# Attention with head mixing and two dense layers: transfer queues of the start, product with v and first dense products moved

## The chip, the cores and the metric

The kernel runs on one core of one Trainium2 chip. The metric is the device time of one execution in microseconds (us); lower is better. TensorE (PE in the profile) has two clock levels, 1.2 and 2.4 GHz; the profile gives the granted clock of a stretch as a share of the higher one.

## The reference

Attention over 2 batches, 12 heads, 448 positions and 64 values per head, with the scores mixed across heads before the softmax and the weights mixed across heads after it; then two dense layers on 896 tokens of 768 values.

```python
scores = scale * np.matmul(q, k.transpose(0, 1, 3, 2))
scores = np.einsum('bhij,hg->bgij', scores, w_pre)
scores = scores - np.max(scores, axis=-1, keepdims=True)
attn = np.exp(scores)
attn = attn / (np.sum(attn, axis=-1, keepdims=True) + 1e-09)
attn = np.einsum('bhij,hg->bgij', attn, w_post)
return np.matmul(attn, v)
...
a = x @ w_a
b = x @ w_b
x = a * b @ w_out
h = x @ w_in
r = np.maximum(h, 0.0)
return (r * r) @ w_out
```

## The kernel before, in words

**Tiles and slots.** A batch is cut into four query tiles of 120, 120, 120 and 88 rows. The scores of a tile are computed per pair of heads (`qk`, line 172) into PSUM, copied to SBUF by ScalarE for even heads and VectorE for odd heads (`qk_copy`, lines 182 and 184), and then moved by transfers from SBUF to SBUF into the buffer `G[t % 2]` (`spread`, lines 192 and 195), where one partition holds one head of one of ten query rows. The attention proper runs in slots of two such groups of rows: six slots for a tile of 120 rows, five for one of 88, 46 slots in all. A slot mixes the heads (`premix`, line 215, out of G), takes the row minimum on VectorE (`smin`, 223) and the exponential on ScalarE (`sexp`, 231), scales the second mixing matrix (`weights2`, 242 to 244), multiplies with it (`post`, 263), and copies the result from PSUM into the tile's buffer A (`evac`, 286 on ScalarE and 284 on VectorE). The product with v (`av`, 298) reads the whole A of a tile, twelve heads in six steps of 16 matmuls; `av_out` (308) copies it to SBUF.

**Order.** The order of every queue is the order of the program text (a manual schedule). In turn n of the slot loop come premix of slot n+1, post of slot n, softmax of slot n+1, evac of slot n, weights2 of slot n+1, then the lists `dve_l` (pieces of the splitting of dense weights) and `mid` (score products of the next tile, splitting of q, k and x, loads, and `av`). The six steps of `av` of a tile lie in the slots of the next tile: two in its second slot, then one a slot. `load_v` of batch 1 stands behind the last `av` of batch 0, and v has one buffer.

**Start.** Tiles 0 and 1 of batch 0 have their scores computed ahead of the loop. Tile 0's scores go to G[0] in three portions, limits GS = (0, 2, 6, 12) groups of rows: transfers of 35, 70 and 105 KB per head. The first two portions are issued by ScalarE's queue (even heads) and SyncE's (odd heads), the third by GpSimd's and SyncE's. Tile 1's scores are staged in `a0`, a tile of the pool "a" (two buffers), and go to G[1] in one transfer of 210 KB per head; each `A[b, t]` is the next tile of the same pool and tag. G[1] is cleared by GpSimd in one memset (322).

**End of attention.** Six steps of the first dense block (each three matmuls, lines 519 to 521) run behind the slot loop, then `attention_tail`: `av` of the last tile, with one PSUM bank "av", and the splitting of batch 1's x (465, 466). The dense part follows.

Of the kernel before, what the change touches and what calls it, by code (L numbers as in the profile page):

```python
# [7 lines left out]
F32 = mybir.dt.float32  # L8
# [7 lines left out]
B, H, S, D = 2, 12, 448, 64  # L16
DM = H * D
# [4 lines left out]
ROW = 2 * KG  # L22
TILE = 120
ROWS = (120, 120, 120, 88)
OFFS = (0, 120, 240, 360)
NTL = 4
PK = 13
GP = 128
JP = 112
NJ = S // JP  # L30
NC = DM // 128
NF1 = DFF1 // 128
NF2 = DFF2 // 128
# [26 lines left out]
def attention_moe_kernel(  # L60
# [18 lines left out]
    def ps(tag):  # L79
        return psum.tile([128, 512], F32, tag=tag, name=tag, bufs=PB[tag])  # L80
# [21 lines left out]
    sb = att.enter_context(tc.tile_pool(name="att", bufs=1))  # L102
    s_p = att.enter_context(tc.tile_pool(name="s", bufs=4))
    e_p = att.enter_context(tc.tile_pool(name="e", bufs=2))
    a_p = att.enter_context(tc.tile_pool(name="a", bufs=2))

    G = [sb.tile([128, H, S], F32, name=f"G{i}") for i in range(2)]
    A = {}
# [43 lines left out]
        qp[b, t] = (hi, lo)  # L152

    def load_v(b, eng=nc.sync):
        x = sb.tile([JP, NJ, DM], F32, tag="v", name="v")
        eng.dma_start(out=x, in_=v[b])
        vv[b] = x

# [28 lines left out]
    def spread(t, h, s, r0, r1, eng=nc.sync):  # L187
        g = G[t % 2]
        n = r1 - r0
        o = r0 * ROW  # L190
        last = ROW - 1 if h == H - 1 else ROW
        eng.dma_start(out=g[h:PK * (last - 1) + h + 1:PK, r0:r1, :], in_=s[o:o + last * n])
        if last < ROW:
            a = place(last, h)
            eng.dma_start(out=g[a:a + 1, r0:r1, :], in_=s[o + last * n:o + ROW * n])
# [15 lines left out]
    def premix(b, m):  # L211
        t, r, n = PAIRS[m]
        for i in range(n):
            p = ps("T")
            nc.tensor.matmul(  # L215
                p[0:GP, 0:S], wpre_sb[0:GP, 0:GP], G[t % 2][0:GP, r + i, :], start=True, stop=True
            )
            Tps[b, m, i] = p

    def smin(b, m, i):  # L220
        if i == 0:
            NB[b, m] = e_p.tile([128, 2], F32, tag="nb", name="nb")
        nc.vector.tensor_reduce(  # L223
            out=NB[b, m][0:GP, i:i + 1], in_=Tps[b, m, i][0:GP, 0:S], op=ALU.min, axis=AX.X
        )

    def sexp(b, m, i):
        if i == 0:
            Z[b, m] = e_p.tile([128, 2], F32, tag="z", name="z")
        e = e_p.tile([128, S], F32, tag=f"e{i}", name="e")  # L230
        nc.scalar.activation(  # L231
            out=e[0:GP], in_=Tps.pop((b, m, i))[0:GP, 0:S], func=ACTF.Exp, bias=NB[b, m][0:GP, i:i + 1], scale=-1.0,
            accum_out=Z[b, m][0:GP, i:i + 1],
        )
        E[b, m, i] = e

    def weights2(b, m):
        n = PAIRS[m][2]
        z = Z.pop((b, m))[0:GP, 0:n]
        NB.pop((b, m))  # L240
        w2 = e_p.tile([128, 2, H * KG], F32, tag="w2", name="w2")
        nc.vector.tensor_scalar(z, z, 1e-9, None, ALU.add)
        nc.vector.reciprocal(out=z, in_=z)
        nc.vector.tensor_tensor(  # L244
            out=w2[0:GP, 0:n, :],
            in0=wp[0:GP].rearrange("p (o g) k -> p o (g k)", o=1).to_broadcast([GP, n, H * KG]),
            in1=z.rearrange("p (n o) -> p n o", o=1).to_broadcast([GP, n, H * KG]), op=ALU.mult,
        )
        W2[b, m] = w2
# [39 lines left out]
    def av(b, t, c):  # L289
        n = ROWS[t]  # L290
        if c % 2 == 0:
            AVp[b, t] = ps("av")
        p = AVp[b, t]
        o = (c % 2) * TILE
        for j in range(NJ):
            for e in range(2):
                g = 2 * c + e
                nc.tensor.matmul(  # L298
                    p[64 * e:64 * e + 64, o:o + n], vv[b][:, j, g * D:(g + 1) * D], A[b, t][:, j * H + g, 0:n],
                    start=(j == 0), stop=(j == NJ - 1), skip_group_check=True,  # L300
                )
# [17 lines left out]
    nc.vector.memset(G[0][:, GS[1]:GS[2], :], 0.0)  # L319
    nc.gpsimd.dma_start(out=wp, in_=wpost)  # L320
    nc.gpsimd.memset(G[0][:, GS[2]:GS[3], :], 0.0)
    nc.gpsimd.memset(G[1], 0.0)
    nc.vector.tensor_scalar(wpre_sb, wpre_sb, -0.125, None, ALU.mult)


# [8 lines left out]
    a0 = a_p.tile([128, NJ * H, TILE], F32, tag="a", name="a0").rearrange("p g i -> p (g i)")  # L334
    stage1 = [a0[0:TILE, h * S:(h + 1) * S] for h in range(H)]
    tags0 = (("qk", "qk"), ("T", "T"), ("post", "post"))
    hw = (nc.scalar, nc.sync)
    for c in range(NC):
        qk(0, 0, c, tags0[c % 3])
        while Sps:  # L340
            _, t, h, p = Sps.pop(0)
            qk_copy(t, h, p, stage0[h])
            spread(0, h, stage0[h], GS[0], GS[1], hw[h % 2])
    for h in range(H):
        spread(0, h, stage0[h], GS[1], GS[2], hw[h % 2])
    load_q(0, 2)
    for h in range(H):
        spread(0, h, stage0[h], GS[2], GS[3], (nc.gpsimd, nc.sync)[h % 2])
    for c in range(NC):
        qk(0, 1, c, tags0[c % 3])  # L350
        while Sps:
            _, t, h, p = Sps.pop(0)
            qk_copy(t, h, p, stage1[h])
    for h in range(H):
        spread(1, h, stage1[h], 0, ROWS[1] // ROW, (nc.gpsimd, nc.sync)[h % 2])
    load_v(0)
    busy(4)

# [3 lines left out]
    span = [sum(1 for x in PAIRS if x[0] == t) for _, t in tiles]  # L362
    base = [sum(span[:i]) for i in range(len(tiles))]
    NS = len(plist)
    act_l, dve_l, mid = {}, {}, {}

    def at(d, slot, *f):
        d.setdefault(max(slot, 0), []).append(f)
# [3 lines left out]
    for ti, (b, t) in enumerate(tiles):  # L372
        s0, sp = base[ti], span[ti]
        if ti + 1 < len(tiles):
            nxt = tiles[ti + 1]
            for c in range(NC if ti else 0):
                at(mid, s0 - 3 + c, qk, *nxt, c)
            if ti + 2 < len(tiles):
                if ti:
                    at(mid, s0 - 2, load_q, *tiles[ti + 2])  # L380
                at(mid, s0 + 1, split_q, *tiles[ti + 2])
            if nxt[1] == NTL - 1 and nxt[0] + 1 < B:
                for i in range(2):
                    at(mid, s0 - 4, load_k, nxt[0] + 1, i)
                for c in range(NC):
                    at(mid, s0 - 2 + c, split_k, nxt[0] + 1, c)
        if ti > 0:
            pb, pt = tiles[ti - 1]
            for c in range(NC):
                s = s0 + 1 + (c * (sp - 1)) // NC  # L390
                at(mid, s, av, pb, pt, c)
                if c % 2:
                    at(mid, s, av_out, pb, pt, c // 2)
            if pt == NTL - 1 and pb + 1 < B:
                at(mid, s0 + sp, load_v, pb + 1)


    NU = w.shape[0]
# [54 lines left out]
    def split_w(u):  # L453
        if u < NU:
            todo.extend(split_steps(u))
# [19 lines left out]

    s0 = base[-1]
    s1 = base[-2]
    at(mid, s1 - 1, load_w, 0)
    at(mid, s1 - 1, load_w, 1)
    at(mid, s1 + 1, split_w, 0)  # L480
    at(mid, s1 + 1, split_w, 1)
    for i in range(12):
        at(dve_l, s1 + 1 + (2 * i) // 3, steps, 1)
    for i in range(NC):
        at(mid, s0 - 1 + (2 * i) // 3, split_x0, i)

    def run(d, n):
        for f in d.get(n, []):
            f[0](*f[1:])

    def softmax(n):
        b, m = plist[n]
        for i in range(PAIRS[m][2]):
            smin(b, m, i)
            sexp(b, m, i)

    premix(*plist[0])
    softmax(0)
    weights2(*plist[0])
    for n in range(NS):  # L500
        if n + 1 < NS:
            premix(*plist[n + 1])
        qk_out()
        post(*plist[n])
        if n + 1 < NS:
            softmax(n + 1)
        run(act_l, n)
        evac(*plist[n], 0)
        evac(*plist[n], 1)
        if n + 1 < NS:  # L510
            weights2(*plist[n + 1])
        run(dve_l, n)
        run(mid, n)
    run(mid, NS)

    def mm(p, u, s, x, first, last):
        hi, lo = whl[u]
# [2 lines left out]
        nc.tensor.matmul(p[:, 0:S], hi[:, sl], x[1], start=False, stop=False)  # L520
        nc.tensor.matmul(p[:, 0:S], lo[:, sl], x[0], start=False, stop=last)  # L521

    tags = ["qk", "T", "post", "av", "qk", "T", "post", "T"]
    tcnt = [0]

    def nps():
# [1 line left out]
        return ps(tags[(tcnt[0] - 1) % 8])  # L528

    soon = []  # L530

    def hook():
        if soon:
            soon.pop(0)()
        else:
            steps(1)


    def stage(u0, order, K, src, consume, first=None):
        acc = {}  # L540
        left = {}
        for u, _ in order:
            left[u] = left.get(u, 0) + 1
        for n, (u, b) in enumerate(order):
            for s in range(US):
                m, k = divmod((u - u0) * US + s, K)
                if k == 0:
                    acc[b, m] = nps()
                mm(acc[b, m], u, s, src[b][k], k == 0, k == K - 1)
                if k == K - 1:  # L550
                    consume(b, m, acc.pop((b, m)))
                hook()
            left[u] -= 1
            if left[u] == 0:
                whl.pop(u)
                split_w(u + 3)
            if first and n == 0:
                first()

    def blocks(u0, nu):  # L560
        return [(u, b) for u in range(u0, u0 + nu) for b in range(B)]
# [61 lines left out]

    order = blocks(0, 2 * NF1)
    order[0:4] = [(0, 0), (1, 0), (0, 1), (1, 1)]
    split_w(2)
    stage(0, order, NC, xs, take_ab, attention_tail)


    ys = [[None] * NC for _ in range(B)]  # L630
# [6 lines left out]

    u1 = 2 * NF1
    n1 = NC * NF1 // US
    stage(u1, blocks(u1, n1), NF1, g1, take_y)  # L640


    g2 = [[None] * NF2 for _ in range(B)]
# [10 lines left out]

    u2 = u1 + n1
    n2 = NC * NF2 // US
    stage(u2, blocks(u2, n2), NC, ys, take_h)

    def take_o(b, m, p):
        o = temp("ta")  # L660
        nc.scalar.copy(o, p[:, 0:S])
        nc.sync.dma_start(out=out[m * 128:(m + 1) * 128, b * S:(b + 1) * S], in_=o)

    stage(u2 + n2, blocks(u2 + n2, n2), NF2, g2, take_o)


def _layout(i):
# [53 lines left out]
```

## Time and profile before

| | |
|---|---|
| median of 3 runs | 763.86 us (762.3 to 764.33) |
| the profiled execution | 763.53 us |
| its span in the trace | 761.7 us |
| PE busy | 740.3 us, 97% |
| VectorE (DVE) busy | 485.7 us, 64% |
| ScalarE (ACT) busy | 316.7 us, 42% |
| GpSimd (POOL) busy | 50.6 us, 7% |
| granted clock of PE, mean | 0.989 |

The span is the trace's own time of one execution; the device time has 1.8 us more around it. Shares are means over stages: the start (to about 34 us), the slots (to about 256 us) and the dense part. SP is SyncE, which only issues transfers; a name with a q behind it (ACTq, SPq, POOLq) is an engine's instruction queue.

### The profile page before, as it was taken

The page shows a single profiled execution, that of the slowest core. Times are in us where ns is not written, and L with a number is a line of the kernel's source. Part 1 is how long each engine was busy: PE and PEld are TensorE (multiplying, and loading weights), DVE is VectorE, ACT ScalarE, POOL GpSimd, SP SyncE. Part 2 cuts the span into 40 slices and gives each one's busy share as a digit, 9 for nine tenths or more (in the row PEclk, how much of TensorE's full clock was granted, in tenths as well). Part 3 has the DMA queues.
Part 4 walks back from the last instruction along what each step waited for, and adds up shares of the span by engine and source line. Part 5 has one row for each costly group of instructions (what it writes and reads, how often), then busy time and mean ns, then how long its engine had stood idle before and what let it go on. Part 6 is the DMA issues. An engine that isn't in the chain of part 4 may idle for free.

```text
span 761.7 us, 12646 instructions
## 1 busy us (share of the span) xinstructions
PE 740.3 (97%) x5113; PEld 624.8 (82%) x5113; DVE 485.7 (64%) x817; ACT 316.7 (42%) x577; POOL 50.6 (7%) x46
## 2 busy tenths in 40 slices
PE   6799999998999999999999999999999999999998
PEld 2466766665677799999999999999999999999997
DVE  4376666564667677676676666566888888654540
ACT  2465655553456343334333332223555554323220
POOL 6230220000004100000000000000000000000000
PEclk9799999998999999999999999999999999999999
DMA  5765332334242123233233333323333233433310
GB/s 188 184 177 161 87 94 90 118 111 140 64 145 64 64 84 125 83 125 123 85 119 106 108 107 118 107 86 122 101 107 125 83 124 103 161 121 141 121 45 34
DMA packets 26967, 84.86 MB, mean 111 GB/s; under 512 B 3454, under 2 KB 16726, under 8 KB 26686
## 3 DMA queue, kind: packets, MB, share of 16 engines
q1 hardware_dynamic: 24910, 80.65, 32.3%
q0 software_dynamic: 800, 1.97, 1.1%
q10 hardware_dynamic: 1200, 1.45, 0.6%
q8 instruction: 40, 0.66, 0.4%
q14 instruction: 17, 0.14, 0.1%
HBM read 62.03 MB, written 2.75 MB: 85 GB/s over the span
## 4 chain that ended last, share of the span: by engine, by line
PE 94%; DMA 2%; DVE 2%; ACTq 1%; ACT 0%; issue 0%; SPq 0%
PE post L263 10%; PE T L215 9%; PE T L519 8%; PE T L521 8%; PE T L520 8%; PE av L298 6%; PE qk L519 5%; PE post L519 5%; PE post L521 5%; PE post L520 5%; PE qk L521 5%; PE qk L520 5%; PE qk L172 4%; PE av L521 3%; PE av L519 3%; PE av L520 3%
## 5 line engine op out<-in xcount | busy, mean ns | idle before, releaser
L443 ACT CAST wh<-wc 128x768 fp32r<-128x768 f32 x68 | 56.8, 835 | 122.3 <-DVE wc L437 108.7
L263 PEld LDWEIGHTS post<-w,e 64*112 64x112 f32 x1440 | 74.4, 174 | 31.6 <-PE T L215 18.2
L448 DVE TENSOR_TENSOR wl<-wc,wh 128x768 fp32r<-128x768 f32 x66 | 63.0, 954 | 48.1 <-ACT wh L443 48.1
L231 ACT ACTIVATE e<-T,nb 128x448 f32<-128x448 f32 x90 | 56.8, 633 | 72.7 <-DVE nb L223 72.6
L520 PE MATMUL T<-m,wh 128*128 128x448 f32 x237 | 86.6, 365 | 0.0
L519 PE MATMUL T<-m,wh 128*128 128x448 f32 x237 | 86.6, 365 | 0.0
L521 PE MATMUL T<-m,wl 128*128 128x448 f32 x237 | 86.5, 365 | 0.0
L263 PE MATMUL post<-w,e 64*112 64x60 f32 x1440 | 80.5, 261 | 2.0 <-DVE w L244 1.8
L215 PE MATMUL T<-G,wpre_sb 128*128 128x448 f32 x180 | 80.3, 568 | 0.0
L426 DVE SCALAR_TENSOR_TENSOR wa<-wr,wa 128x768 uint32<-128x768 uint32 x68 | 65.2, 958 | 2.3
L437 DVE SCALAR_TENSOR_TENSOR wc<-wc,wa 128x768 uint32<-128x768 uint32 x68 | 65.1, 958 | 2.3
L223 DVE TENSOR_REDUCE nb<-T 128x1 f32<-128x448 f32 x90 | 55.3, 621 | 13.1 <-PE T L215 9.5
L284 DVE COPY a<-post 112x480 f32<-112x480 f32 (+1 forms) x46 | 30.8, 670 | 49.1 <-PE post L263 47.9
L421 ACT ACTIVATE wc<-wr 128x768 f32<-128x768 f32 x68 | 61.3, 902 | 0.0
L215 PEld LDWEIGHTS T<-G,wpre_sb 128*128 128x128 f32 x180 | 30.6, 190 | 28.2 <-issue 26.7
L298 PE MATMUL av<-a,v 112*64 112x120 f32 (+1 forms) x768 | 46.8, 270 | 6.0 <-DMA v<-v 3.8
L433 DVE TENSOR_SCALAR wc<-wc 128x768 f32<-128x768 f32 x68 | 38.6, 568 | 16.3 <-ACT wc L421 16.3
L298 PEld LDWEIGHTS av<-a,v 112*64 112x64 f32 x768 | 38.4, 140 | 12.4 <-DMA v<-v 4.2
L521 PEld LDWEIGHTS T<-m,wl 128*128 128x128 f32 x237 | 44.5, 188 | 3.5
L520 PEld LDWEIGHTS T<-m,wh 128*128 128x128 f32 x237 | 44.5, 188 | 3.5
L519 PEld LDWEIGHTS T<-m,wh 128*128 128x128 f32 x237 | 44.5, 188 | 3.5
L422 DVE TENSOR_SCALAR wa<-wr 128x768 uint32<-128x768 uint32 x68 | 39.2, 576 | 0.0
(162 smaller groups left out, 1421.8 us busy)
## 6 DMA issues: line engine op xcount, KB each, us to landing
wr<-w SPq DMA_DIRECT2D x68, 768.0 KB
G<-s SPq DMA_DIRECT2D x44, 210.0 KB
G<-s SPq DMA_DIRECT2D x22, 140.0 KB
k<-kT SPq DMA_DIRECT2D x12, 224.0 KB
v<-v SPq DMA_DIRECT2D x2, 1344.0 KB
outT<-ta SPq DMA_DIRECT2D x12, 224.0 KB
q<-qT SPq DMA_DIRECT2D x6, 360.0 KB
G<-a POOLq DMA_DIRECT2D x6, 210.0 KB, 8.6
```

What stands on the lines that cost most here:

```text
L215: nc.tensor.matmul(p[0:GP, 0:S], wpre_sb[0:GP, 0:GP], G[t % 2][0:GP, r + i, :], start=True, stop=True)
L231: nc.scalar.activation(out=e[0:GP], in_=Tps.pop((b, m, i))[0:GP, 0:S], func=ACTF.Exp, bias=NB[b, m][0:GP, i:i + 1], scale=-1.0, accum_out= ...
L263: nc.tensor.matmul(p[f][0:JP, c:c + k], e[o:o + 64, j * JP:(j + 1) * JP], w2[o:o + 64, i, :], start=True, stop=True,)
L298: nc.tensor.matmul(p[64 * e:64 * e + 64, o:o + n], vv[b][:, j, g * D:(g + 1) * D], A[b, t][:, j * H + g, 0:n], start=(j == 0), stop=(j == ...
L421: nc.scalar.activation(out=st["c"], in_=rd(st["high"]), func=ACTF.Abs, scale=HSC)
L426: nc.vector.scalar_tensor_tensor(out=a, in0=st["high"], scalar=0x80000000, in1=a, op0=ALU.bitwise_and, op1=ALU.bitwise_or)
L437: nc.vector.scalar_tensor_tensor(out=cu, in0=cu, scalar=3, in1=st["a"], op0=ALU.logical_shift_left, op1=ALU.bitwise_or)
L443: nc.scalar.copy(st["hi"], st["c"])
L448: eng.tensor_tensor(out=lo, in0=st["c"], in1=rd(st["hi"]), op=ALU.subtract)
L519: nc.tensor.matmul(p[:, 0:S], hi[:, sl], x[0], start=first, stop=False)
L520: nc.tensor.matmul(p[:, 0:S], hi[:, sl], x[1], start=False, stop=False)
L521: nc.tensor.matmul(p[:, 0:S], lo[:, sl], x[0], start=False, stop=last)
```

## The change

Tile 0's first two portions are issued by GpSimd's queue instead of ScalarE's for even heads, and the load of q for tile 2 comes behind the third portion on SyncE's queue instead of ahead of it. The memset of G[1] is shared by VectorE and GpSimd. Pool "a" has one buffer and v has two; v of batch 1 is loaded in batch 0's third tile. The six steps of `av` of a tile stand together at the end of the tile's own last slot, and its middle pair of steps uses a bank of "post". Loads and splitting of dense weights begin earlier and cover three units; ten steps of the first dense products lie in the last five slots, two in each, and one ahead of the attention's tail.

```diff
-    a_p = att.enter_context(tc.tile_pool(name="a", bufs=2))
+    a_p = att.enter_context(tc.tile_pool(name="a", bufs=1))
...
-        x = sb.tile([JP, NJ, DM], F32, tag="v", name="v")
+        x = sb.tile([JP, NJ, DM], F32, tag="v", name="v", bufs=2)
...
-            AVp[b, t] = ps("av")
+            AVp[b, t] = ps("post" if c == 2 else "av")
...
-    nc.gpsimd.memset(G[1], 0.0)
+    nc.vector.memset(G[1][:, 0:6, :], 0.0)
+    nc.gpsimd.memset(G[1][:, 6:H, :], 0.0)
...
-    hw = (nc.scalar, nc.sync)
+    hw = (nc.gpsimd, nc.sync)
...
-    for h in range(H):
-        spread(0, h, stage0[h], GS[1], GS[2], hw[h % 2])
+    for i in range(1, 3):
+        for h in range(H):
+            spread(0, h, stage0[h], GS[i], GS[i + 1], hw[h % 2])
     load_q(0, 2)
-    for h in range(H):
-        spread(0, h, stage0[h], GS[2], GS[3], (nc.gpsimd, nc.sync)[h % 2])
...
-        spread(1, h, stage1[h], 0, ROWS[1] // ROW, (nc.gpsimd, nc.sync)[h % 2])
+        spread(1, h, stage1[h], 0, ROWS[1] // ROW, hw[h % 2])
...
-        if ti > 0:
-            pb, pt = tiles[ti - 1]
+        if ti + 1 < len(tiles):
             for c in range(NC):
-                s = s0 + 1 + (c * (sp - 1)) // NC
-                at(mid, s, av, pb, pt, c)
+                at(end, s0 + sp - 1, av, b, t, c)
                 if c % 2:
-                    at(mid, s, av_out, pb, pt, c // 2)
-            if pt == NTL - 1 and pb + 1 < B:
-                at(mid, s0 + sp, load_v, pb + 1)
+                    at(end, s0 + sp - 1, av_out, b, t, c // 2)
+        if t == 1 and b + 1 < B:
+            at(mid, s0 + sp, load_v, b + 1)
...
-    at(mid, s1 - 1, load_w, 0)
-    at(mid, s1 - 1, load_w, 1)
-    at(mid, s1 + 1, split_w, 0)
-    at(mid, s1 + 1, split_w, 1)
-    for i in range(12):
-        at(dve_l, s1 + 1 + (2 * i) // 3, steps, 1)
-    for i in range(NC):
-        at(mid, s0 - 1 + (2 * i) // 3, split_x0, i)
...
+    at(mid, s1 - 8, load_w, 0)
+    at(mid, s1 - 8, load_w, 1)
+    for u in range(3):
+        at(mid, s1 - 5, split_w, u)
+    for i in range(18):
+        at(dve_l, s1 - 4 + (2 * i) // 3, steps, 1)
+    for c in range(NC):
+        at(mid, s1 - 2 + c, split_x0, c)
...
-    split_w(2)
-    stage(0, order, NC, xs, take_ab, attention_tail)
+
+    gated = stage(0, order, NC, xs, take_ab)
+
+    def fill(n):
+        for _ in range(n):
+            next(gated)
...
     for n in range(NS):
         if n + 1 < NS:
             premix(*plist[n + 1])
+        if n >= s0:
+            fill(2)
         qk_out()
         post(*plist[n])
...
         run(mid, n)
+        run(end, n)
+
+    fill(1)
+    attention_tail()
+    filling[0] = False
+    for _ in gated:
+        pass
```

`stage` becomes a generator that stops behind every step; while `filling` is set it does not call `hook`. Here `s0` is the first slot of the last tile and `s1` that of the tile before it; in the loop over tiles `s0` and `sp` are a tile's first slot and its number of slots.

## Rows read from the trace of the kernel before

**Rows 1.** The page's part 1: busy time, share of the span, instructions.

```profile
PE 740.3 (97%) x5113; PEld 624.8 (82%) x5113; DVE 485.7 (64%) x817; ACT 316.7 (42%) x577; POOL 50.6 (7%) x46
```

**Rows 2.** Windows by stretch: length, busy time of each engine, clock, DMA share, GB/s.

```profile
10.00:20.00 10.00, 5.06 (x24) 2.27 (x20) 3.75 (x6) 1.81 (x4) 2.40 (x5) 0.86 0.51 150
...
180.00:220.00 40.00, 36.48 (x394) 25.54 (x396) 21.34 (x51) 16.80 (x39) 1.70 (x1) 0.91 0.35 109
235.00:257.00 22.00, 21.21 (x275) 16.08 (x274) 15.57 (x37) 13.60 (x30) 9.95 (x8) 1.00 0.11 37
...
266.00:740.00 474.00, 474.00 (x2341) 439.23 (x2340) 325.73 (x455) 180.94 (x269) 0.00 (x0) 1.00 0.32 110
```

**Rows 3.** Waits of PE: total us, times, longest us.

```profile
PE qk L172 <- ACT a L184: 6.4, 1, 6.4
PE av L298 <- DMA v<-v: 3.8, 1, 3.8
PE av L298 <- DVE x L308: 2.2, 4, 0.6
PE post L263 <- DVE w L244: 1.8, 2, 1.4
```

**Rows 4.** Timeline of the start: start us, us, engine, line, operation.

```profile
4.52 4.60 POOL L322 MEMSET G<- 128x5376 f32 x1
6.38 2.82 DVE L323 TENSOR_SCALAR wpre_sb<-wpre_sb 128x128 f32<-128x128 f32 x1 [3.61 <-DMA wpre_sb<-wpre]
...
15.27 4.86 SPq L192 DMA_DIRECT2D G<-x  x6
15.39 6.83 ACTq L192 DMA_DIRECT2D G<-x  x7
```

**Rows 5.** The chain that ended last, from 0 to 45 us.

```profile
11.05 0.75 PE post L172 x4
...
34.13 1.70 PE T L215 x4
35.84 1.71 PE post L263 x32
```

**Rows 6.** Transfers of G into SBUF, 0 to 22 us: issues on GpSimd, then landing.

```profile
L192 POOL DMA_DIRECT2D G<-x x6: 553/556/587, 9.0 to 15.7; - x6
...
DMA to landing us min/median/max: 2.3/2.5/2.7
```

**Rows 7.** Queues from 25 to 34 us: packets, MB, share; q0 is GpSimd's, q1 SyncE's.

```profile
q0 software_dynamic: 438, 1.24, 66.5%
q1 hardware_dynamic: 312, 0.48, 21.5%
```

**Rows 8.** The same view from 34.5 to 42 us.

```profile
q1 hardware_dynamic: 875, 1.63, 69.4%
```

**Rows 9.** Timeline behind the first post: its copy, and weights2 of the next slot.

```profile
34.21 0.68 DVE L284 COPY a<-post 112x480 f32<-112x480 f32 x1 [0.85 <-PE post L263]
...
35.17 0.28 DVE L244 TENSOR_TENSOR w<-wp,z 128x120 f32<-128x120 f32 x1
```

**Rows 10.** The chain where v of batch 1 is awaited.

```profile
183.52 3.47 PE av L298 x32
186.99 2.14 PE T L215 x4
```

**Rows 11.** The chain from 60 to 76 us, slots with steps of av.

```profile
62.80 1.79 PE av L298 x32
...
68.01 0.66 PE qk L172 x6
68.67 0.97 PE av L298 x16
...
74.03 0.77 PE qk L172 x6
```

**Rows 12.** Timeline behind the last av: splitting of batch 1's x.

```profile
266.11 3.30 DVE L466 TENSOR_TENSOR m<-x,m 128x448 fp32r<-128x448 f32 x6 [0.30 <-ACT m L465]
```

More of the change, by code (lines that the diff above doesn't have):

```diff
@@ L364, in attention_moe_kernel @@
     NS = len(plist)
-    act_l, dve_l, mid = {}, {}, {}
+    dve_l, mid, end = {}, {}, {}
     def at(d, slot, *f):
@@ L477, in attention_moe_kernel @@
     s1 = base[-2]
-    at(mid, s1 - 1, load_w, 0)
-    at(mid, s1 - 1, load_w, 1)
-    at(mid, s1 + 1, split_w, 0)
-    at(mid, s1 + 1, split_w, 1)
-    for i in range(12):
-        at(dve_l, s1 + 1 + (2 * i) // 3, steps, 1)
-    for i in range(NC):
-        at(mid, s0 - 1 + (2 * i) // 3, split_x0, i)
[L487 to L514, printed above, removed]
+    at(mid, s1 - 8, load_w, 0)
[6 more added lines that the diff above has]
+        at(mid, s1 - 2 + c, split_x0, c)
     def mm(p, u, s, x, first, last):
@@ L521, in mm @@
         nc.tensor.matmul(p[:, 0:S], lo[:, sl], x[0], start=False, stop=last)
-    tags = ["qk", "T", "post", "av", "qk", "T", "post", "T"]
+    tags = ["qk", "qk", "T", "post", "av", "T", "post", "T"]
     tcnt = [0]
@@ L530, in attention_moe_kernel @@
     soon = []
+    filling = [True]
     def hook():
@@ L536, in hook, with stage @@
             steps(1)
-    def stage(u0, order, K, src, consume, first=None):
+    def stage(u0, order, K, src, consume):
         acc = {}
@@ L551, in stage @@
                     consume(b, m, acc.pop((b, m)))
-                hook()
+                yield
+                if not filling[0]:
+                    hook()
             left[u] -= 1
@@ L556, in stage @@
                 split_w(u + 3)
-            if first and n == 0:
-                first()
     def blocks(u0, nu):
@@ L625, in attention_moe_kernel, with run, softmax @@
     order[0:4] = [(0, 0), (1, 0), (0, 1), (1, 1)]
-    split_w(2)
-    stage(0, order, NC, xs, take_ab, attention_tail)
+    gated = stage(0, order, NC, xs, take_ab)
+    def fill(n):
+        for _ in range(n):
+            next(gated)
+    def run(d, n):
+        for f in d.get(n, []):
+            f[0](*f[1:])
+    def softmax(n):
+        b, m = plist[n]
+        for i in range(PAIRS[m][2]):
+            smin(b, m, i)
+            sexp(b, m, i)
+    premix(*plist[0])
+    softmax(0)
+    weights2(*plist[0])
+    for n in range(NS):
+        if n + 1 < NS:
+            premix(*plist[n + 1])
+        if n >= s0:
+            fill(2)
+        qk_out()
+        post(*plist[n])
+        if n + 1 < NS:
+            softmax(n + 1)
+        evac(*plist[n], 0)
+        evac(*plist[n], 1)
+        if n + 1 < NS:
+            weights2(*plist[n + 1])
+        run(dve_l, n)
+        run(mid, n)
+        run(end, n)
[4 more added lines that the diff above has]
+        pass
     ys = [[None] * NC for _ in range(B)]
@@ L639, in attention_moe_kernel @@
     n1 = NC * NF1 // US
-    stage(u1, blocks(u1, n1), NF1, g1, take_y)
+    for _ in stage(u1, blocks(u1, n1), NF1, g1, take_y):
+        pass
     g2 = [[None] * NF2 for _ in range(B)]
@@ L656, in attention_moe_kernel @@
     n2 = NC * NF2 // US
-    stage(u2, blocks(u2, n2), NC, ys, take_h)
+    for _ in stage(u2, blocks(u2, n2), NC, ys, take_h):
+        pass
     def take_o(b, m, p):
@@ L662, in take_o @@
         nc.sync.dma_start(out=out[m * 128:(m + 1) * 128, b * S:(b + 1) * S], in_=o)
-    stage(u2 + n2, blocks(u2 + n2, n2), NF2, g2, take_o)
+    for _ in stage(u2 + n2, blocks(u2 + n2, n2), NF2, g2, take_o):
+        pass
 def _layout(i):
```

## The prediction

> **What bounds the kernel now.** I began with the busy shares: PE works 97% of the span, so at most 21.4 us can be won, and an engine off PE's path matters only where PE waits for it [rows 1]. The windows show where those 21 us lie. The dense part has no gap at all, 474.00 of 474 us busy, so nothing is to be had behind 266 us. The gaps are in the start (5.06 of 10 us busy, clock 0.86) and around 180 us (36.48 of 40, clock 0.91) [rows 2]. The waits give causes: 6.4 us for a ScalarE copy in the start, 3.8 us for v, 2.2 us in four waits for the copy behind av [rows 3]. The 6.4 us are ScalarE's seven transfer issues, 6.83 us from 15.39 on, ahead of the copies that free PSUM [rows 4]. A wait also costs clock: behind the one for v, 32 matmuls of av took 3.47 us and a premix 2.14 [rows 10], against 1.79 [rows 11] and 1.70 [rows 5]: 2.1 us more, at the lower of the two levels. That is nowhere in PE's idle time.
>
> **The start.** ScalarE loses its twelve issues, so the twelve score steps of tiles 0 and 1 can follow each other at 0.75 us [rows 5] and end near 15 us. Premix of slot 1 needs the second portion: SyncE's issues cost 0.81 us each [rows 4], two portions are 14 issues from about 7.5, so about 19, and with 2.5 us to landing [rows 6] 21.5. Were that all, post of slot 0 and premix of slot 2, at 34.13 before [rows 5], would come some 6 to 8 us earlier.
>
> It isn't all. `a0`, which stages tile 1's scores, and `A[0, 0]` are tiles of one pool and tag, and the pool now has one buffer. The first evac writes where the transfers of tile 1 still read, so it waits until all twelve of 210 KB are through, and they are the last of both queues. Before, A had the other buffer. Behind evac of slot 0 on VectorE stands weights2 of slot 1, so post of slot 1 waits too; PE gets no further than premix of slot 2.
>
> When is tile 1 through? Each queue carries 0.215, 0.43, 0.645 and 1.29 MB (six heads of 35, 70, 105, 210 KB), SyncE's also q with 0.37 MB ahead of tile 1. GpSimd is free at 4.52 + 4.60/2 = 6.8 [rows 4]; its first portion is paced by the copies to about 11.5, and the 18 issues behind it at 0.56 us [rows 6] are made by 22, faster than the data moves. Where both queues were full, GpSimd's moved 1.24 MB and SyncE's 0.48 MB in 9 us, 138 and 53 GB/s [rows 7]; alone, SyncE's moved 1.63 MB in 7.5 us, 217 GB/s [rows 8]. So GpSimd's remaining 2.37 MB take 17.2 us, to 28.7. SyncE's, from 12.6 on, has by then moved 0.85 MB of its second and third portions' 1.08; the 0.23 left, q and tile 1 are 1.89 MB, 8.7 us: 37.4, say 37.5. From the start of an evac to the end of weights2 is 34.21 to 35.45, 1.24 us [rows 9]. Post of slot 1 then starts at 38.8 instead of 35.84 [rows 5]: 3.0 us later. PE has been idle for some 10 us by then, and the lower clock takes 2.1 us as worked out above. **Start: +5.1 us.**
>
> Bounds: all 5.53 MB at 217 GB/s from 7.2 on would end at 32.7, +0.3 in all; an end at 42, where the stretch of rows 8 with the old tile 1 ends, gives +9.6. I take the sum by queue, since rows 7 show the same mixture of transfers. The memset on VectorE (half of G[1], no such row) costs between 2.3 us (GpSimd's rate) beside GpSimd's, and a wait to 6.8 and 2.3 more. VectorE already waited to 9.20 for the whole memset [rows 4], so at worst little changes; either way the wait for tile 1 hides it. The q load goes behind seven more issues and is hidden too, as its splitting stands behind the same evac on ScalarE. v of batch 0 goes out at about the same place in the queue; its use comes later.
>
> **v of batch 1.** With two buffers it is loaded two tiles ahead. The 3.8 us wait [rows 3] and 2.1 us of clock go: **−5.9 us**; nothing is late next, as A and G of that slot are ready. At least 3.8 of it is certain.
>
> **av in one run.** Two steps together take 1.79 us, one alone 0.97 [rows 11], so a further step in a run costs 0.82. Before: 1.79 + 4 × 0.97 = 5.67 a tile; in a run 0.97 + 5 × 0.82 = 5.07. That is 0.6 a tile, 4.2 in seven tiles. A qk behind av takes 0.77, otherwise 0.66 [rows 11]: three a tile in six tiles, 2.0. Against it, av now waits for the last evac of its own tile, a copy of 0.68 us [rows 9] begun as post ends; the qk of 0.66 between covers all but about 0.2, six times 1.2, and the last but one tile has no qk there: 0.85. Together **−4.1 us**. If only the pairs' overhead were apparent, it would be +2.
>
> **Slots without av.** Slots lose 0.97 us of PE work that covered VectorE, and six more pieces of weight splitting fall into tiles 5 to 7, where GpSimd is busy 9.95 of 22 us [rows 2]. VectorE's small steps have been held long enough to cost PE 1.4 us once [rows 3]. I estimate **+2.0** (one such wait and 0.6 spread), bounds 0 and +4.
>
> **Tail and fill.** A second bank for av removes the 2.2 us of waits [rows 3]. But only one dense step, 3 × 474/2341 = 0.61 us [rows 2], now separates av from batch 1's x, where there were six; the first copy and subtract need about 1.2, the following ones 0.55 each [rows 12], less than a step: +0.6. The eleven dense steps put ahead are moved, not saved: PE idles only 0.8 us from 235 to 257 [rows 2], and 0.6 of that is counted already. **−1.6 us.**
>
> **Sum:** +5.1 − 5.9 − 4.1 + 2.0 − 1.6 = −4.5 us on the profiled execution's 763.53, so 759.0. The median of the runs lies 0.3 above that execution: 759.4.
>
> **Rivals.** (1) The wait for `a0` doesn't bind, since something releases the tile early; the start then gains about 6 us and the whole comes to 748. For it: the large part of the wait is only read from the text, no trace row shows it. Against it: the evac would overwrite what the transfers still read. Chance 0.10.
>
> (2) Tile 1 lands no earlier than before, at 42: the start costs 9.6, and the sum is zero, 763.9. For it: the DMA share of 0.88 in 25 to 34 us, 66.5 + 21.5% [rows 7]. Against it: from 10 to 20 us the share was 0.51 [rows 2], so there is room to fill. The Trainium skill, DMA: Bandwidth & Descriptors, section "Issuing engines are not separate DMA queues", says that transfers from all engines run on the same 16 DMA engines and that another issuing engine saves issue time only. By that rule moving the queue alone wins nothing, this rival; the trace agrees for 25 to 34 us and not for 10 to 20. Chance 0.15.
>
> (3) Slower: GpSimd's queue crowds SyncE's out. If SyncE moved nothing while GpSimd's 2.37 MB went, to 28.7, then its 2.74 MB behind the first portion would take 12.6 us, to 41.3; with GpSimd at 100 instead of 138 GB/s it is 47.8, the start costs 15.4, and the whole 769.6. It decides from a landing of tile 1 at about 44.5 on, where the sum is +2.5. For it: 138 against 53 GB/s [rows 7]. Against it: 53 isn't zero. Chance 0.08.
>
> (4) The slots become bound by VectorE and GpSimd, and av in a run and the slots without it cancel at zero: 761.5. Chance 0.07.
>
> **How the numbers follow.** The forecast has 0.60. About 0.3%, 2.3 us, is what a measurement of this kernel can tell from no change, so faster means below 761.6. Forecast mostly (0.57), rival 1 and a part of rival 4 are faster: 0.70. Rival 2, the rest of 4 and the forecast's upper end are the same: 0.21. Rival 3 with (2)'s upper end is slower: 0.09. The range takes the bounds of the start around the forecast (754.6 to 763.9) and rival 2, leaving out rivals 1 and 3: 754.5 to 764.5.
>
> **What would show it.** Right: the first ACT and DVE evac wait for a transfer G<-a until about 37.5, PE is idle from about 27 to 38 at a falling clock and post of slot 1 starts near 39; score steps end near 15; no wait for v near 183; av in groups of 96 matmuls of about 5.1 us; a wait of some 0.6 us behind the last av. Wrong: an evac at 27 or before (rival 1), a landing of tile 1 past 41 (2, 3), or waits of post for w in many slots (4).

## The result and the profile after

The changed kernel takes **770.74 us** (median of 8 runs, 766.97 to 774.41) against 763.86 (8 runs, 762.3 to 764.41): ratio 1.0092, 95% interval [1.0063, 1.0121]. It is slower by 0.9%, where 759.4 was forecast. Here and below, medians and ranges are of all runs; ratios and intervals leave out the few that took over 1.5% longer than the fastest of their kernel. The profiled execution took 769.13 us, its span is 767.3, 5.6 us more than before.

PE's busy time in the page's first part answers [rows 1]: 740.3 before, for the same 5113 matmuls. So the added time is idle time in sum. Busy time counts a matmul at either clock level, so what the lower one costs has to be read from durations.

```profile
PE 740.2 (96%) x5113; PEld 627.6 (82%) x5113; DVE 484.4 (63%) x818; ACT 314.1 (41%) x577; POOL 54.2 (7%) x58
```

The windows show where (columns as in [rows 2]).

```profile
41.00:53.00 12.00, 11.82 (x71) 8.51 (x72) 5.00 (x14) 6.92 (x16) 6.96 (x6) 0.50 0.18 51
...
30.00:40.00 10.00, 3.19 (x10) 1.44 (x8) 0.22 (x1) 0.24 (x1) 0.00 (x0) 0.67 0.73 235
...
180.00:220.00 40.00, 38.76 (x487) 28.58 (x487) 26.73 (x58) 19.68 (x47) 5.72 (x4) 1.00 0.38 123
220.00:246.00 26.00, 22.86 (x246) 15.37 (x246) 20.80 (x45) 15.07 (x36) 6.91 (x5) 0.93 0.31 98
...
280.00:740.00 460.00, 460.00 (x2271) 426.38 (x2270) 319.20 (x445) 174.79 (x257) 0.00 (x0) 1.00 0.33 112
```

The dense part is full, as before. The stretch around 180 us has recovered from clock 0.91 to 1.00. Two stretches are new: PE is busy for only 3.19 of 10 us from 30 on, then works from 41 to 53 at a granted clock of 0.50, the level of 1.2 GHz; and from 220 to 246 it stands for 3.1 us in all, at a mean clock of 0.93. PE's waits name the causes (total, times, longest, in us; compare [rows 3]).

```profile
PE post L263 <- DVE w L244: 10.2, 2, 8.0
PE T L215 <- DMA G<-a: 6.0, 1, 6.0
PE T L215 <- DMA G<-s: 1.9, 3, 0.8
PE av L298 <- DVE z L242: 1.7, 4, 0.9
...
PE av L298 <- ACT a L286: 0.7, 2, 0.6
```

The 6.4 us for a ScalarE copy, the 3.8 for v and the 2.2 in the tail are gone. In their place stand 10.2 us for the weights w, in two waits, 6.0 us of premix of slot 1 for transfers into G, and small new ones for the next tile's scores (G<-s) and ahead of av. The chain of waits for the start and for tiles 5 and 6 (start us, us, what):

```profile
19.74 4.04 DMA G<-a
...
23.95 3.33 PE T L215 x4
27.28 3.23 PE post L263 x32
...
30.71 0.79 SPq L192
...
35.91 3.75 DMA G<-a
...
40.75 0.29 DVE w L244
...
41.18 3.25 PE post L263 x32
44.43 3.28 PE T L215 x4
47.71 3.18 PE post L263 x32
50.89 2.76 PE T L215 x4
53.65 1.72 PE post L263 x32
...
201.74 4.38 DMA G<-s
...
210.84 1.86 PE av L298 x32
212.70 1.64 PE post L298 x32
214.34 1.64 PE av L298 x32
215.98 1.70 PE T L215 x4
...
235.64 1.78 PE post L263 x32
237.42 3.29 PE T L215 x4
```

The first wait ends at 23.78; premix of slot 1 reads the second portion of tile 0, whose last issue by SyncE ended at 19.72. PE works at the lower level behind it, but waits again until 41 in any case. Post of slot 1, at 35.84 before [rows 5], starts at 41.18. From there a slot of post and premix costs 6.5 us instead of 3.4, until 53.65. The six steps of av stand together at 210.84, 5.14 us in all. The timeline gives what holds the two waits for w (start us, us, engine, line, operation, idle time before and its releaser).

```profile
39.76 0.64 ACT L286 COPY a<-post 112x480 f32<-112x480 f32 x1 [11.06 <-DMA G<-a]
39.78 0.68 DVE L284 COPY a<-post 112x480 f32<-112x480 f32 x1 [11.84 <-DMA G<-a]
...
232.45 1.82 POOL L446 TENSOR_TENSOR wl<-wc,wh 128x768 fp32r<-128x768 f32 x1
...
232.98 1.31 DVE L242 TENSOR_SCALAR z<-z 128x2 f32<-128x2 f32 x1 [0.67 <-ACT e L231]
...
234.23 1.13 POOL L471 TENSOR_TENSOR ks<-x,ks 128x448 fp32r<-128x448 f32 x1
...
234.53 0.97 DVE L244 TENSOR_TENSOR w<-wp,z 128x120 f32<-128x120 f32 x1
```

The first is the predicted one: both evacs stand idle until G<-a has landed. The second is in tile 6: two small VectorE steps, which take 0.15 and 0.28 us elsewhere (0.28 in [rows 9]), take 1.31 and 0.97 and end within 0.2 us of a GpSimd instruction (234.27, 235.36). The Trainium skill, SBUF — State Buffer, section "Who interferes with whom", has VectorE and GpSimd share a pair of ports as an exclusive lock; these rows agree.

To compare kernels stage by stage, here is where post of some slots starts in each profiled execution, in us, from PE's timelines. Slots count from 0; tiles 1 to 7 begin with slots 6, 12, 18, 23, 29, 35 and 41. With av at the end of its tile, a kernel has one tile's av more behind it at slots 35 and 41 than the others have; with early dense steps it has 2 of them (1.2 us) behind it at slot 41 and 10 at slot 45.

| kernel | 0 | 3 | 5 | 35 | 41 | 45 | span |
|---|---|---|---|---|---|---|---|
| before | 32.35 | 44.04 | 52.19 | 209.58 | 237.65 | 254.49 | 761.7 |
| after | 27.21 | 53.58 | 61.74 | 217.61 | 251.34 | 267.64 | 767.3 |
| 1: after, two buffers for a | 28.06 | 40.34 | 48.50 | 208.61 | 243.97 | 260.28 | 760.0 |
| 2: after, added matmuls | 28.79 | 56.65 | 64.81 | 221.37 | 255.13 | 271.44 | 780.8 |
| 3: before, early v | 31.48 | 45.95 | 54.10 | 205.56 | 233.65 | 250.49 | 757.6 |
| 4: before, new start | 27.93 | 40.27 | 48.44 | 204.79 | 232.86 | 249.70 | 757.1 |
| 7: before, 3 and 4 | 28.82 | 40.50 | 50.27 | 201.72 | 229.81 | 246.64 | 754.1 |
| 5: 7 and av in a run | 28.26 | 39.93 | 49.71 | 204.61 | 234.09 | 249.60 | 756.5 |
| 6: 1 with av spread | 30.43 | 41.81 | 49.98 | 201.43 | 230.99 | 252.69 | 754.7 |
| 8: 1, splitting on VectorE | 28.74 | 40.45 | 50.22 | 209.00 | 245.64 | 261.95 | 761.6 |
| 9: before, av in a run | 31.92 | 43.60 | 51.75 | 205.80 | 236.85 | 252.82 | 760.5 |
| 10: 7, run in third slot | 28.72 | 43.31 | 53.08 | 199.66 | 227.74 | 248.63 | 755.3 |
| 11: 7, added matmuls | 30.29 | 44.95 | 54.73 | 206.18 | 234.26 | 251.10 | 757.2 |
| 12: 11, five tiles in a run | 26.36 | 40.72 | 48.89 | 195.47 | 223.56 | 240.40 | 746.5 |

After against before: +9.5 us at slot 3; +8.0 at slot 35, with a run of 5.1 us more done, so +2.9; +13.69 at slot 41, less 5.14 and 1.22, so +7.3; +13.15 at slot 45, where it has 10 dense steps (6.1) and one step of av (1.0) more done, so +6.1; +5.6 at the end. The start loses 9.5, the slots to 35 win 6.6 (5.9 of it v), tile 6's slots lose 4.4, the rest wins 1.7.

### The profile page after: what moved, and what is told of

Same layout as the page of the kernel before. It is cut to its first block, busy times and chain, and to the rows that moved or that the text cites. A ratio compares the mean times of both kernels' runs of the same rounds, so it can differ in the third digit from the quotient of the medians.

```text
span 767.3 us, 12663 instructions
## 1 busy us (share of the span) xinstructions
PE 740.2 (96%) x5113; PEld 627.6 (82%) x5113; DVE 484.4 (63%) x818; ACT 314.1 (41%) x577; POOL 54.2 (7%) x58
## 4 chain that ended last, share of the span: by engine, by line
PE 90%; DMA 3%; DVE 2%; issue 1%; POOL 1%; ACT 1%; SPq 1%; DVEq 0%; ACTq 0%
PE post L263 9%; PE T L215 9%; PE T L489 8%; PE T L490 8%; PE T L488 8%; PE post L489 5%; PE post L490 5%; PE post L488 5%; PE qk L488 5%; PE qk L490 5%; PE qk L489 5%; PE av L298 3%; PE av L489 3%; PE av L488 3%; PE av L490 3%; PE qk L172 2%
## 5 line engine op out<-in xcount | busy, mean ns | idle before, releaser
L263 PEld LDWEIGHTS post<-w,e 64*112 64x112 f32 x1440 | 78.7, 183 | 40.7 <-PE T L215 16.3
L263 PE MATMUL post<-w,e 64*112 64x60 f32 x1440 | 84.9, 270 | 10.2 <-DVE w L244 10.2
L215 PE MATMUL T<-G,wpre_sb 128*128 128x448 f32 x180 | 86.9, 607 | 7.8 <-DMA G<-a 6.0
L489 PE MATMUL T<-m,wh 128*128 128x448 f32 x213 | 77.9, 366 | 0.2 <-DVE m L464 0.2
L488 PE MATMUL T<-m,wh 128*128 128x448 f32 x213 | 77.9, 366 | 0.0
L490 PE MATMUL T<-m,wl 128*128 128x448 f32 x213 | 77.8, 365 | 0.0
L215 PEld LDWEIGHTS T<-G,wpre_sb 128*128 128x128 f32 x180 | 32.8, 204 | 39.0 <-issue 33.1
L489 PE MATMUL post<-m,wh 128*128 128x448 f32 x125 | 45.6, 365 | 0.0
L490 PE MATMUL post<-m,wl 128*128 128x448 f32 x125 | 45.6, 365 | 0.0
L488 PE MATMUL post<-m,wh 128*128 128x448 f32 x125 | 45.6, 365 | 0.0
L489 PEld LDWEIGHTS T<-m,wh 128*128 128x128 f32 x213 | 40.0, 188 | 3.6 <-DVE m L464 0.5
L488 PEld LDWEIGHTS T<-m,wh 128*128 128x128 f32 x213 | 40.0, 188 | 3.4 <-ACT m L463 0.3
L490 PEld LDWEIGHTS T<-m,wl 128*128 128x128 f32 x213 | 40.0, 188 | 3.1
```

Source lines behind the costliest of these rows:

```text
L215: nc.tensor.matmul(p[0:GP, 0:S], wpre_sb[0:GP, 0:GP], G[t % 2][0:GP, r + i, :], start=True, stop=True)
L263: nc.tensor.matmul(p[f][0:JP, c:c + k], e[o:o + 64, j * JP:(j + 1) * JP], w2[o:o + 64, i, :], start=True, stop=True,)
L488: nc.tensor.matmul(p[:, 0:S], hi[:, sl], x[0], start=first, stop=False)
```

## The experiments

The theory: the shared buffer of pool "a" causes the first loss, and av in a run at the end of its tile the second, as it leaves slots with too little PE work to cover VectorE. The rivals: the start loses because transfers are slower, buffer or not; the early weight splitting, not the moved av, causes the second loss.

**1. Two buffers for a.**

```diff
-    a_p = att.enter_context(tc.tile_pool(name="a", bufs=1))
+    a_p = att.enter_context(tc.tile_pool(name="a", bufs=2))
```

> The changed kernel with two buffers in pool a again, all else as changed. Theory (the staging tile shared with A holds the first evac until the last transfer of tile 1 has landed, at 39.7 us in the changed trace, and the idle time costs clock behind it): the first evac follows the first post at once, post of slot 1 starts near 33 us instead of 41.2, the start comes out some 10 us earlier, about 760 us. Rival (the transfers themselves bind the start, whichever buffer they are read from): the wait moves to a later slot of tile 0 and the time stays above 766.

Measured: 761.74 us (10 runs, 756.9 to 774.87), ratio to before 0.9968 [0.9947, 0.999]. That is 9.0 us under the changed kernel. Slot 3 comes at 40.34 instead of 53.58. Its chain and waits:

```profile
34.26 1.74 PE T L215 x4
36.00 1.77 PE post L263 x32
```

```profile
PE T L215 <- DMA G<-x: 7.9, 2, 7.2
PE T L215 <- DMA G<-s: 3.3, 3, 2.0
PE post L263 <- DVE w L244: 3.1, 2, 2.2
```

The wait of 8.0 us for w is gone, and premix and post run at 1.7 us there. So the shared buffer did it, and with two buffers the new queues win 3.7 us by slot 3. The rival that the start loses by slower transfers falls. What remains is a wait of premix for tile 0's own portions (7.2). Of the 13.2 us won by slot 3, 4.0 go again in slots 10 and 11, which take 18.34 us instead of 14.31: the tile's transfers come due earlier, and a wait of 2.0 us for G<-s is followed by the lower clock.

**2. Matmuls without use, to hold the clock.** In the changed kernel, 24 ahead of premix of slot 1 and 34 behind that of slot 2.

```diff
+        if n == 0:
+            busy(24)
         if n + 1 < NS:
             premix(*plist[n + 1])
+        if n == 1:
+            busy(34)
```

> The changed kernel with 24 dummy products between premix of slot 0 and of slot 1 and 34 between premix of slot 2 and post of slot 1, in the two stretches where PE waited 6.0 and 8.0 us; they end before the waits do. Theory (a part of the loss is the lower clock behind the waits, 12.5 us from post of slot 1 to post of slot 3 against 6.8 us of work): the clock stays at its higher level, post of slot 3 comes some 5 us earlier, about 764 to 765 us. Rival (the lower clock comes of the kind of work in the slots and not of the idle time): no change, or up to 1 us more.

Measured: 775.18 us (5 runs, 774.78 to 782.53), ratio 1.016 [1.0143, 1.0177]: slower, a miss. Tile 1 landed at 42.6 in its profile instead of 39.66, the 34 matmuls had ended by 38.9, and post of slot 1 took 3.25 us all the same. So work measured out for one landing didn't cover a later one; it says nothing against the clock as a part of the loss. The profile is of the longest execution, 782.53 us. Behind slot 45 it takes 9.6 us more than the changed kernel: in the dense part PE, without a wait and at a granted clock of 1.00, makes 243 to 244 matmuls in 50 us where the changed kernel made 248 to 249. Why is open; the added matmuls have all ended by 39 us.

**3. Early v alone.** Before, with two buffers for v and its load in the third tile.

```diff
-        x = sb.tile([JP, NJ, DM], F32, tag="v", name="v")
+        x = sb.tile([JP, NJ, DM], F32, tag="v", name="v", bufs=2)
```

> The kernel before with v in two buffers and its second load two tiles ahead, alone. Theory (the term of the prediction): 3.8 us of wait and 2.1 us of clock go, 5.9 us less, 758 us. Rival (the wait hides another one, for G or for the softmax of the next slot): 2 to 4 us less.

Measured: 757.6 us (4 runs, 757.28 to 759.53), 0.9937 [0.9921, 0.9953]: 5.8 us, as forecast (5.9). From slot 5 to 35 the profile takes 151.46 us instead of 157.39, 5.9 less.

**4. The new start alone, with two buffers for a.**

```diff
-    hw = (nc.scalar, nc.sync)
+    hw = (nc.gpsimd, nc.sync)
```

(and the order of the portions, of q and of the memset as in the change)

> The kernel before with the new start alone (queues, order of the q load, memset shared), pool a with two buffers as it was. Theory (only the shared buffer makes the new start slow): premix of slot 1 waits for the second portion until about 24 us at a falling clock, post of slot 1 comes near 33 instead of 35.8, 3 to 4 us less, 760 us. Rival (the new queues are the loss: the second portion and tile 1 land later): no gain, 764 us or more.

Measured: 760.28 us (10 runs, 759.31 to 765.78), 0.9977 [0.9959, 0.9995]: 3.1 us less, 3.8 by slot 3 in the profile. Premix of slot 1 waits 7.1 us for the second portion there. Most of the 6.4 us wait of [rows 3] has come back as this one.

**7. Early v and the new start** (the edits of 3 and 4).

```diff
+        if t == 1 and b + 1 < B:
+            at(mid, s0 + sp, load_v, b + 1)
...
-    hw = (nc.scalar, nc.sync)
+    hw = (nc.gpsimd, nc.sync)
```

> The kernel before with the new start and v loaded early, nothing else. Both terms alone were 5.8 and 3.1 us; theory (they are apart in time and add up): 754.5 us. Rival (an earlier start brings the slots closer to their transfers of G and gives a part back): 756 to 758 us.

Measured: 757.68 us (6 runs, 754.24 to 761.55), 0.9935 [0.9903, 0.9968]. Together they win 7.9 us by slot 35 in the profile (4.0 and 4.8 alone), and 5.8 in the median instead of 8.9, so the rival's range holds. A part of the rest is in slot 3, 5.70 us instead of 4.07: behind a wait of 1.4 us for w premix takes 3.0 us at the lower level. Before and in experiment 4 the same wait was followed by the higher one. Its runs spread over 7 us, those of experiment 3 over 2.

**5. The same with av in a run, without the early splitting and dense steps.**

```diff
-            AVp[b, t] = ps("av")
+            AVp[b, t] = ps("post" if c == 2 else "av")
...
-                at(mid, s, av, pb, pt, c)
+                at(end, s0 + sp - 1, av, b, t, c)
```

> The kernel before with the new start, v loaded early and av of a tile in one run, pool a with two buffers; the dense weights split and the first dense products placed as before. Theory (the early splitting is what crowds VectorE and GpSimd in tile 6, some 6 us with the clock that the wait costs): about 6 us less than the changed kernel with two buffers, 755 to 756 us. Rival (the loss is that of short slots without av, whatever is split in them): 760 us or more.

Measured: 764.07 us (10 runs, 758.28 to 770.78), 0.9997 [0.9969, 1.0025]: 6.4 us more than 7 in the medians, 4.7 by the ratios. So the run of av loses without any early splitting. The profile, 758.28 us, is of its fastest execution and shows the smaller part of this.

**6. The changed kernel with two buffers and av spread as before**, early splitting and dense steps kept (the diff of 5, undone on 1):

```diff
-            AVp[b, t] = ps("post" if c == 2 else "av")
+            AVp[b, t] = ps("av")
...
-                at(end, s0 + sp - 1, av, b, t, c)
+                s = s0 + 1 + (c * (sp - 1)) // NC
+                at(mid, s, av, pb, pt, c)
```

> The changed kernel with two buffers in pool a and av spread over the slots of the next tile again, the early splitting and the dense products in the last slots kept. Theory (slots with av in them cover both the transfers of G and VectorE's work): no wait for G, no wait for w in tile 6, 753 to 755 us. Rival (the early splitting crowds the slots in any case): 758 us or more.

Measured: 757.71 us (4 runs, 755.86 to 759.77), 0.9929 [0.9906, 0.9951]: 4.0 us less than 1, and the same as 7; 753 to 755 was expected. The wait for G<-s is gone from PE's list and that for w is 0.2 us. Early splitting and dense steps cost nothing where av is spread: the rival that blames them for the loss falls. Beside av in a run they do shift it: from slot 35 to 41 the changed kernel takes 32.5 us without its two dense steps, 5 takes 29.5 and 9 takes 31.05, and a wait of 0.7 us for G<-s in slot 33, where an early load of weights stands between SyncE's issues, is in the changed kernel and in neither of 5 and 9. Tile 7 gives this back.

**8. The GpSimd part of the splitting on VectorE** (two buffers, av in a run).

```diff
-            eng = nc.gpsimd if u < 2 else nc.vector
+            eng = nc.vector
```

> The changed kernel with two buffers in pool a, and the low parts of the first two weight units subtracted on VectorE instead of GpSimd. Theory (VectorE's small steps in tile 6 wait for GpSimd's subtractions, which starts a wait of 2.2 us and a fall of the clock): the wait of post for w in slot 39 shrinks below 1 us and the clock doesn't fall, 756 to 758 us. Rival (VectorE has simply too much to do there): the same 761 to 762 us or more.

Measured: 760.54 us (10 runs, 755.4 to 766.75), 0.9965 [0.9941, 0.999], no different from 1. The wait for w in slot 39 is 0.4 us instead of 2.2, so GpSimd's work beside VectorE's small steps made most of it. But slot 40 takes 14.83 us instead of 10.92: premix of slot 41 now waits for the last scores of tile 7, and the lower clock follows (timeline as above):

```profile
228.88 2.00 PE L215 MATMUL T<-G,wpre_sb 128*128 128x448 f32 x4 [1.88 <-DMA G<-s]
230.81 3.25 PE L263 MATMUL post<-w,e 64*112 64x60 f32 x32
```

SyncE's issues for one head of tile 7 take 0.80 and 1.22 us, two heads a slot, so 4.0 us of a slot of 4.05. Without av the slots are as short as the issuing of the next tile's transfers. So what GpSimd does to VectorE is one bound of these slots, and the transfers are the next, close behind it.

**9. Only av in a run, on the kernel before** (with the second bank of 5, and the load of v behind the run).

```diff
-                at(mid, s, av, pb, pt, c)
+                at(end, s0 + sp - 1, av, b, t, c)
...
-            if pt == NTL - 1 and pb + 1 < B:
-                at(mid, s0 + sp, load_v, pb + 1)
+        if t == NTL - 1 and b + 1 < B:
+            at(mid, s0 + sp, load_v, b + 1)
```

> The kernel before, with the six steps of av in one run at the end of their own tile and nothing else (v of batch 1 then loads behind the run of batch 0's last tile, a tile ahead of its use, so its wait must go with it: -5.8 us as measured). If the run itself is worth what was forecast, 763.5 - 5.8 - 4.1 = 753.6 us. If the slots that lose av become bound by VectorE's chain of small steps, as the runs with and without the run at the new start say (+4 to +6 us), 761.7 to 763.7 us, with waits of PE's post for w in slots of tiles 6 and 7, and the slot of the run at 9.4 us.

Measured: 766.98 us (12 runs, 760.87 to 773.29), 1.0039 [1.0007, 1.0071]: above both expectations; the profiled execution, 762.73, lies in the second. Why the median lies 4 us above it was not found. The chain in the last slots of tile 6 and in tile 7:

```profile
218.03 1.76 PE post L263 x32
...
219.82 0.69 DVE a L284
...
220.79 0.28 DVE w L244
221.07 0.87 DVE wa L424
221.94 0.47 DVE wc L431
222.41 0.55 DVE nb L223
...
223.04 1.35 ACT e L231 x4
...
224.81 0.28 DVE w L244
225.09 0.87 DVE wc L435
...
228.52 3.42 PE av L298 x32
...
243.09 0.28 DVE w L244
...
248.06 0.29 DVE w L244
```

From the w of slot 39 to that of slot 40 this chain takes 4.0 us (220.79 to 224.81), in tile 7 from slot 43 to 44 5.0 (243.09 to 248.06), with pieces of weight splitting (wa, wc) between w and the row minimum nb. Slots 38, 41 and 42 are not bound by it and take 3.42 us. PE has post and premix there, 3.4 us: no tile follows whose scores are still to be computed, and av has left. The run itself then waits 1.5 us for the last evac and starts at the lower clock, 3.42 us for 32 matmuls; most of tile 6's loss is in this slot. With one step of av a slot the same slots of experiment 7 take 4.39 us, all PE's work. By the table, slots 35 to 41 take 31.05 us here and 28.07 before, with one tile's av in both: 3.0 us lost. In slots 41 to 45, 15.97 against 16.84 that held five steps of av (4.9): 4.0 lost. From slot 5 to 35, where score products remain, the run wins: 154.05 less its additional run of 5.14 against 151.46 in experiment 3, 2.5 us or 0.5 a tile.

**10. The run in the third slot of the next tile** (on 7, with the second bank of 5).

```diff
-                s = s0 + 1 + (c * (sp - 1)) // NC
+                s = s0 + 2
                 at(mid, s, av, pb, pt, c)
```

> New start with two buffers and early v (757.7 us), with the six steps of av in one run, but in the third slot of the tile behind instead of at the end of their own. If only the place of the run costs (the next tile's transfers and the last evac of the same tile come due too early), this keeps the forecast gain of 0.6 us a tile: 753.5 us and no wait for G<-s. If the other slots suffer because they have lost av, wherever the run stands, it comes out like the run at the end: 761 to 764 us, with waits of post for w.

Measured: 757.19 us (6 runs, 752.83 to 765.42), 0.9908 [0.9882, 0.9934]: between the two. From slot 5 to slot 35 it takes 146.58 us and experiment 7 151.45: 4.87, or **0.97 us a tile**, with no wait for G<-s. At the end of the tile the same run gave 0.5. Behind that it gives the gain back: slots 35 to 41 win nothing (28.08 us against 28.09), and from slot 41 to 45 it takes 20.89 us with six steps in a run against 16.83 with five spread. So there are two costs: the place, in every tile, and the emptied slots, in tiles 6 and 7.

**11. Matmuls without use in the start, and a second bank for the tail** (on 7).

```diff
-            AVp[b, t] = ps("av")
+            AVp[b, t] = ps("post" if c == 2 and (b, t) == (B - 1, NTL - 1) else "av")
...
+        if n == 0:
+            busy(24)
```

> New start with two buffers and early v (757.7 us), 24 matmuls without use ahead of the premix of slot 1, and a second PSUM bank for the last tile's av. If the lower clock behind the start's idle time comes from that idle time, the first premix and posts run at the higher level and save 1.5 to 3 us; the second bank saves the 2.2 us of waits for the copy behind av: 752.5 to 754 us. If the clock does not follow the added matmuls, only the tail gains: 755.5 us.

Measured: 754.01 us (6 runs, 750.64 to 759.33), 0.9885 [0.9857, 0.9914]. The mean granted clock is 0.995 to 0.999 in five of the six and 0.986 to 0.995 in the runs of 7, which fits added matmuls that hold it in most. It isn't shown apart: the tail's bank was changed with them and took 0.9 of the 2.2 us of waits behind av (1.3 are left), and no trace of those five was kept. The profile is of the sixth, 759.33 us:

```profile
27.04 3.33 PE T L215 x4
30.36 3.18 PE post L263 x32
33.54 3.22 PE T L215 x4
```

There the transfers landed at 26.8, PE waited 3.5 us in spite of them, and premix and post ran at the lower level until 36.75.

**12. The same with av in a run in the third slot for tiles 0 to 4 alone.**

```diff
+            run = b * NTL + t not in (5, 6)
+            AVp[b, t] = ps("post" if c == 2 and run else "av")
...
-                s = s0 + 1 + (c * (sp - 1)) // NC
+                s = s0 + 2 if ti < 6 else s0 + 1 + (c * (sp - 1)) // NC
```

> The kernel with the added matmuls and the tail's second bank (754.0 us), with av in one run in the third slot of the tile behind for tiles 0 to 4 alone; tiles 5 and 6 keep their steps spread. If av in a run is worth what was forecast as long as the slots that it leaves have other PE work and no weight splitting, five tiles give 0.6 + 2/6 = 0.93 us each, 4.7 us: 749.3 us, with no wait of post for w beyond the one of the start. If the run costs wherever it stands, 754 us or more.

Measured: **752.39 us** (6 runs, 748.65 to 754.19), 0.9849 [0.9809, 0.9889], faster than both kernels. From slot 5 to 35 it takes 146.58 us against 151.45, the same 4.87 as in 10, and from slot 41 to 45 16.84, what spread av takes. The median gains 1.6 us on 11 and the ratio 2.7, less than the profile's part; the rest stays open. The profile is of its fastest execution, 748.65 us, so its span isn't the gain. Its timeline has premix and post at the higher level behind a wait of 2.4 us:

```profile
24.69 1.74 PE L215 MATMUL T<-G,wpre_sb 128*128 128x448 f32 x4 [2.41 <-DMA G<-x]
26.36 1.78 PE L263 MATMUL post<-w,e 64*112 64x60 f32 x32
```

## Why the prediction was wrong

**Start: the mechanism was right, its size was not.** +5.1 was forecast, +9.5 came by slot 3. Score steps end near 15 as written, and both evacs wait for G<-a. Tile 1 landed at 39.66, not 37.5, and post of slot 1 started at 41.18, not 38.8: 2.4 us. The sum went by bytes; the chain ahead of the landing is SyncE's issues of tile 1, from 30.71 on, some 0.8 us each. The larger part is the term "the lower clock takes 2.1 us as worked out above". It was taken from one instance, the 32 matmuls of av and one premix behind the wait for v. Here two posts and two premixes ran at or near the lower level: 12.47 us from 41.18 to 53.65 for 6.85 us of work, so 5.6, against which before had its 1.4 us wait for w in that place. The forecast took the duration of the lower clock from one row; [rows 10] bound it only for that wait. Rival (2) gave 9.6 for the start, by a later landing; its size came, its landing at 42 did not. The gain without the shared buffer, "some 6 to 8 us", was 3.7 to 3.8 by slot 3 (experiments 1 and 4): the second portion, forecast for 21.5, was in at about 23.8 and later, some 4 us behind its last issue where the sum had 2.5.

**v: right.** -5.9 forecast, -5.8 in experiment 3.

**av in one run: the place was wrong.** "0.6 a tile" and the dearer qk were right: experiments 10 and 12 give 0.97 a tile where 0.6 + 2.0/6 = 0.93 was forecast. The step that put only 0.2 a tile against it was wrong for the end of the tile. With short slots of 4.1 us, the run put behind them, the next tile's transfers come due earlier, and PE waits for G<-s (3 waits, 1.9 us) and for z and a ahead of av (2.4 us). In the changed kernel tiles 0 to 4 gave 155.87 - 5.14 = 150.73 us from slot 5 to 35 against 151.46 in experiment 3: 0.7 us in five tiles, where the terms make 0.73 a tile.

**Slots without av: right in kind, too small.** "+2.0" was one wait and a little; tile 6's slots lost 4.4 us in the profile, 3.0 with the run alone (9). The estimate looked at single VectorE steps held by GpSimd, and such steps do make most of the wait of 2.2 us in slot 39 (8). What it left out is what else stands close behind: the whole chain from w over the splitting pieces, minimum and exponential to the next w, 4.0 to 5.0 us in slots of 9, against 3.4 us of PE work where neither av nor score products are left; the transfers of the next tile (8); and the clock that falls behind such waits. This chain could have been added up from the kernel before. Rival (4) named this bound, but let it cancel the gain and no more. By size the start missed by 4.4 us, the run by 3 (0.7 where five tiles make 3.7) and these slots by 2.4.

**Tail and fill: the sum was right.** -1.6 forecast; tile 7 and the tail win 1.7 in the profile, 1.2 of it by slot 45 and 0.4 behind, where the second bank was to win the most. So the agreement is in part luck. The wait behind the last av is 0.2 instead of 0.6. The dense steps cover tile 7's emptied slots, which lost 4.0 in experiment 9; the forecast had counted them as moved only.

In medians: start with two buffers -3.1, shared buffer +9.0, v -5.8, av in a run +4.0 (1 against 6) to +6.4 (5 against 7). These don't add up exactly, as 7 shows. The slower rival (3) doesn't hold: tile 1 landed at 39.66, below its 44.5, and two buffers took the loss away with the same queues.

## What to carry to other kernels

Before a pool loses a buffer, list every tile that lives in it with its last reader, transfers too: here one buffer tied the first copy of the slots to the last transfers of the start. Before work is gathered into one run, add up the chain of the other engines in the slots that it leaves, and the issuing of transfers too: if that is longer than the PE work that stays, the gathered work was cover; gather it where other work remains, and in the middle of a tile. And price a wait on PE with the clock behind it as a range from several waits, not with one row.

## What the runs showed of the hardware

How long PE runs at the lower level behind an idle stretch differs much. Before, it was the av and one premix behind the wait for v [rows 10]. In the changed kernel it lasted from 41.18 to about 53, with PE busy for 11.82 of the 12 us. In experiment 12 premix after a wait of 2.4 us, with matmuls without use ahead of it, was at the higher level at once; after a second wait of 2.4 us, with premix and post ahead of it, it took 2.94 us, mostly at the lower one. The landing of the same twelve transfers of tile 1 differed by 3 us between the changed kernel and experiment 2 (39.66 and 42.6), and the last of tile 0's transfers on GpSimd's queue landed between 22.2 us (experiment 1) and 27.2 us (experiment 6), with the same start in both.
